# Attention weights all in two halves, the threshold on ScalarE, and a new order of the attention's operations

## The chip, the core and the metric

The kernel runs on one core of a Trainium2 chip. The metric is the device time of one execution in microseconds (us), here the median of several. The core has TensorE (PE; its weight loads are listed apart as PEld), VectorE (DVE), ScalarE (ACT), GpSimd (POOL) and SyncE (SP, which here only issues transfers).

## What is computed

The reference has three stages: attention in which only scores close to the row's largest one count, a mixture of experts that gives each token to one expert, and a feed-forward layer. The change is in the attention.

```python
def _attn_ref(q, k, v, tau) -> np.ndarray:      # (4, 8, 576, 64) each
    scale = 1.0 / np.sqrt(q.shape[-1])
    scores = scale * np.matmul(q, k.transpose(0, 1, 3, 2))
    thresh = np.max(scores, axis=-1, keepdims=True) - tau
    scores = np.where(scores >= thresh, scores, -1000000000.0)
    scores = scores - np.max(scores, axis=-1, keepdims=True)
    attn = np.exp(scores)
    attn = attn / (np.sum(attn, axis=-1, keepdims=True) + 1e-09)
    return np.matmul(attn, v).astype(np.float32)
...
    attn_out = _attn_ref(**attn_kwargs)
    x = np.ascontiguousarray(attn_out.transpose(0, 2, 1, 3)).reshape(B * S, H * D)
    x = _moe_ref(x=x, **moe_kwargs)
    return _moe2_ref(x=x, **moe2_kwargs)
```

## The kernel before

The attention works in 16 pairs: a pair is one head of two of the four batch rows, 2 x 576 = 1152 queries, cut into nine tiles of 128 (tile 4 holds 64 queries of each row and needs twice the products). For each tile `qk` puts the negated, scaled scores s (128 x 576) into one of two score buffers in PSUM; `smin` takes the least of each row on VectorE (column 0 of a small tile mx, whose column 1 holds tau); `sthr` adds tau to it (column 2); `sexp` makes e = exp(least - s) on ScalarE; `smask` on VectorE keeps e where s is at most column 2, writes the weights p and sums each row. The score buffer is free when the mask is done.

TensorE then turns p by 128 x 128 transposes into a PSUM bank t (`ptr`; two banks, for one or two tiles at a time). From there the turned weights go to SBUF (`evac`) and are multiplied with v (`pv`, four products a pair, each 288 queries wide, one bank v). A product in float32r is made exact enough by two halves: hi is the value rounded, lo is what the rounding dropped, and v has its two halves side by side as the stationary operand `hlv`, so that one pass with `pth` (hi) and one with `ptl` (lo) multiply all of it. The keys come in five blocks, four of 128 and one of 64. In the kernel before, `NAT = (1, 1)` says that one 128-key block of each batch row is not split: it stays float32 in the tile `pt` and is multiplied as a whole float32 product with the unsplit `rawv`. The other blocks' halves are made in one of three ways: hi by ScalarE and lo by VectorE from PSUM; a copy to SBUF (tile x) by ScalarE and both halves on GpSimd, for the groups that `VIA` names; or, for the second block, both halves on GpSimd from `pt`. The 64-key block keeps its two halves in `pt4`. `oout` copies a product's result to o, and `fin` folds the two halves of v and adds the experts' logits; `fin_l` and `fin_x` scale them by the row sums.

The order of all this is not the order of the code. `pair` hands every operation to a planner (`Plan`) with its engine, a cost, its dependencies, the buffers that it takes and a rank; the planner lists them by earliest start, and among equals by rank. The numbers of `BIAS` (by kind of operation) and `BIASP` (by kind and pair) are added to the ranks. Each engine then works through its own list in that order. After the last pair the routing follows (`pick`, `count`, `slot`, and `scatter`, which writes the tokens to the experts' rows), and after it the experts and the feed-forward layer, which the change doesn't touch.

Of the kernel before, what the change touches and what calls it, by code (L numbers as in the profile page):

```python
# [16 lines left out]
ALU = mybir.AluOpType  # L17
# [135 lines left out]
def attn_moe_ffn(ctx: ExitStack, tc, q, k, v, tau, emb, mtau, w1, w2, w_in, w_out, alpha, out):  # L153
# [192 lines left out]
    COL = [0, 256, 512, 640, 896]  # L346
    PQ = []

    def load(pr, nm):
# [212 lines left out]
    C0 = min(NAT)  # L562

    def dst(pr, tag):
        st = PQ[pr]
        if tag not in st:
            shp = {"pt": [128, 2, 2 * S], "pt4": [128, 2 * S]}.get(tag, [128, 4 - C0, 2 * S])
            st[tag] = new(tag, shp, F32 if tag == "pt" else F32R)
        return st[tag]

    def evac(pr, g, chunks, what):
# [12 lines left out]
        v = m[:, 0:len(chunks) * n].rearrange("p (c j) -> p c j", c=len(chunks))  # L584
# [1088 lines left out]
```

## Time and profile before

| | us |
|---|---|
| median of three executions | 1065.36 (1065.16 to 1066.11) |
| profiled execution, its own time | 1063.56 |
| span from its first to its last instruction | 1061.4 |
| busy in the span: TensorE | 1008.0 (95%) |
| VectorE | 708.5 (67%) |
| ScalarE | 507.6 (48%) |
| GpSimd | 529.0 (50%) |

The attention takes about the first 375 us of the span, the routing, the experts and the feed-forward layer the rest. Busy time is the time in which an engine has at least one instruction under way; a TensorE that is busy can have instructions that wait for one another. A share of the whole span mixes stages, so the rows further down are cut by stage.

### The profile page before, as it was taken

Reading aid. Unit: us, or ns where it says so; the run is one execution under the profiler, and the core shown is the slowest. Engines: PE = TensorE matmul, PEld = TensorE weight load, DVE = VectorE, ACT = ScalarE, POOL = GpSimd, SP = SyncE. Lnnn points to the kernel's source line nnn. Section 1 sums busy time; section 2 is a strip of 40 time slices with the busy share of each in tenths; the row PEclk is TensorE's granted clock in tenths of the full one; section 3 lists DMA queues with packets and bytes.
Section 4 is the critical chain, followed back from the end, with each engine's and each line's share of the span. In section 5 each row is a group of like instructions: output and inputs, shape, how many; then the busy total and the mean of one; then the engine's idle time right before and its main releaser. Section 6 shows DMA issues by size and latency. Waiting matters only on the chain. (4 is left out here: it accounts for less than half of the span.)

```text
span 1061.4 us, 17732 instructions
## 1 busy us (share of the span) xinstructions
PE 1008.0 (95%) x6224; PEld 908.6 (86%) x6224; DVE 708.5 (67%) x1501; ACT 507.6 (48%) x1074; POOL 529.0 (50%) x610
## 2 busy tenths in 40 slices
PE   7999999999999849999999997999999999999995
PEld 6888888878888738999999996999999999999995
DVE  8988888898889747787868887889642222422321
ACT  5777777788777534555546553232231111311112
POOL 6688786888886432222355223756533222332223
PEclk9999999999999979999999998999999999999998
DMA  4265564433321066686988854222220000000001
GB/s 117 66 186 164 155 170 139 120 116 89 80 67 40 1 200 226 191 266 180 242 204 195 246 166 111 80 63 77 80 90 30 1 1 1 31 30 1 1 1 63
DMA packets 100098, 113.67 MB, mean 107 GB/s; under 512 B 22072, under 2 KB 81464, under 8 KB 100000
## 3 DMA queue, kind: packets, MB, share of 16 engines
q1 hardware_dynamic: 96544, 102.99, 34.5%
q0 software_dynamic: 3456, 9.46, 2.4%
q8 instruction: 51, 0.84, 0.3%
q14 instruction: 47, 0.39, 0.1%
HBM read 75.21 MB, written 28.36 MB: 98 GB/s over the span
## 5 line engine op out<-in xcount | busy, mean ns | idle before, releaser
L1560 POOL TENSOR_TENSOR gl<-t,gh 128x384 fp32r<-128x384 f32 x96 | 102.5, 1068 | 246.5 <-ACT gh L1559 246.5
L1556 DVE TENSOR_SCALAR t<-h,alpha_t 128x384 f32<-128x384 f32 x96 | 59.1, 616 | 206.2 <-PE h L1554 200.7
L1559 ACT CAST gh<-t 128x384 fp32r<-128x384 f32 x96 | 49.3, 513 | 271.3 <-DVE t L1557 162.8
L530 DVE TENSOR_REDUCE mx<-s 128x1 f32<-128x576 f32 x144 | 108.1, 754 | 25.5 <-PE s L523 24.1
L546 DVE SCALAR_TENSOR_TENSOR p<-s,mx,e 128x576 f32<-128x576 f32 x144 | 115.9, 810 | 10.8 <-ACT e L539 7.8
L539 ACT ACTIVATE e<-s,mx 128x576 f32<-128x576 f32 x144 | 107.2, 746 | 14.9 <-DVE mx L530 13.6
L1004 DVE TENSOR_TENSOR w<-stg,w 128x512 fp32r<-128x512 f32 x128 | 107.8, 858 | 9.1 <-ACT w L1003 8.5
L1572 PE MATMUL o<-wo,gl 128*128 128x512 f32 x288 | 113.3, 394 | 0.0
L1571 PE MATMUL o<-wo,gh 128*128 128x512 f32 x288 | 113.1, 393 | 0.0
L1570 PE MATMUL o<-wo,gh 128*128 128x512 f32 x288 | 112.3, 390 | 0.0
L559 PE MATMUL t<-ident,p 128*128 128x128 f32 (+1 forms) x720 | 107.6, 277 | 3.6 <-DVE ptl L377 1.1
L559 PEld LDWEIGHTS t<-ident,p 128*128 128x128 f32 (+1 forms) x720 | 80.9, 137 | 7.5 <-ACT pt L586 3.4
L523 PE MATMUL s<-ks,qs 128*128 128x288 f32 x256 | 80.6, 330 | 6.2 <-DVE p L546 5.3
L1003 ACT CAST w<-stg 128x512 fp32r<-128x512 f32 x128 | 76.7, 619 | 15.8 <-DMA stg<-in_moe_w_dram 15.8
L1097 PE MATMUL y<-h,w 128*128 128x256 f32 (+6 forms) x256 | 80.2, 313 | 2.8 <-DVE h L1065 2.8
L1096 PE MATMUL y<-h,w 128*128 128x256 f32 (+6 forms) x256 | 82.3, 321 | 0.0
L1060 PE MATMUL l<-x,w 128*128 128x256 f32 (+6 forms) x256 | 79.8, 312 | 0.3 <-DVE x L1048 0.2
L1059 PE MATMUL l<-x,w 128*128 128x256 f32 (+6 forms) x256 | 79.9, 312 | 0.0
L1098 PE MATMUL y<-h,w 128*128 128x256 f32 (+6 forms) x256 | 79.6, 311 | 0.0
L1061 PE MATMUL l<-x,w 128*128 128x256 f32 (+6 forms) x256 | 79.5, 310 | 0.0
L523 PE MATMUL s<-kx,qs 128*128 128x288 f32 x256 | 72.9, 299 | 0.2
L1554 PE MATMUL h<-yh,wi_b 128*128 128x384 f32 x216 | 73.0, 338 | 0.0
(233 smaller groups left out, 2756.1 us busy)
## 6 DMA issues: line engine op xcount, KB each, us to landing
stg<-in_moe_w_dram SPq DMA_DIRECT2D x64, 512.0 KB, 5.4
kx<-ks SPq DMA_DIRECT2D x60, 144.0 KB, 2.5
xd<-zt SPq DMA_DIRECT2D x8, 1024.0 KB, 7.5
raw<-in_moe_w_in_dram SPq DMA_DIRECT2D x16, 512.0 KB, 3.7
raw<-in_moe_w_out_dram SPq DMA_DIRECT2D x16, 512.0 KB, 3.5
rawk<-in_k_dram SPq DMA_DIRECT2D x16, 256.0 KB, 2.9
rawq<-in_q_dram SPq DMA_DIRECT2D x16, 256.0 KB, 2.9
yd<-zt SPq DMA_DIRECT2D x4, 1024.0 KB, 6.8
```

What stands on the lines that cost most here:

```text
L523: nc.tensor.matmul(s[:, hf, 0:288], lt, st[nm, a][:, hf * 288:(hf + 1) * 288], start=(j == 0 and x == 0), stop=(j == n - 1 and x == 1))
L530: nc.vector.tensor_reduce(out=mx[:, 0:1], in_=st["s", t][:, :, 0:288], op=ALU.min, axis=AX.XY)
L539: nc.scalar.activation(e, st["s", t][:, :, 0:288], AF.Exp, bias=st["mx", t][:, 0:1], scale=-1.0)
L546: nc.vector.scalar_tensor_tensor(out=p.rearrange("q (a b) -> q a b", a=2), in0=st["s", t][:, :, 0:288], scalar=st["mx", t][:, 2:3], in1=st ...
L559: nc.tensor.transpose(m[0:w, j * n + i * 128:j * n + (i + 1) * 128], st["p", t][:, c * 128:c * 128 + w], ident)
L1004: nc.vector.tensor_tensor(t[:, 1], src, t[:, 0].bitcast(F32), op=ALU.subtract)
L1096: nc.tensor.matmul(m[:, 0:n], w[:, 0, dsl], h[:, 0, 0:n], start=(f == 0), stop=False)
L1097: nc.tensor.matmul(m[:, 0:n], w[:, 0, dsl], h[:, 1, 0:n], start=False, stop=False)
L1560: nc.gpsimd.tensor_tensor(gl, g, gh.bitcast(F32), op=ALU.subtract)
L1570: nc.tensor.matmul(m, gh[:, ts], WO[f][:, 0, :], start=(f == 0), stop=False)
L1571: nc.tensor.matmul(m, gh[:, ts], WO[f][:, 1, :], start=False, stop=False)
L1572: nc.tensor.matmul(m, gl[:, ts], WO[f][:, 0, :], start=False, stop=(f == KF2 - 1))
```

## The change

All four 128-key blocks of a batch row are now split, so `pt` and the product with `rawv` are gone: a product is nine passes of the same kind. Each transposed bank of 128 x 512 is one unit; the nine units of a pair are named A to I, and B, D, E, G and I are copied by ScalarE and split on GpSimd in every pair, while A, C, F and H have hi from ScalarE and lo from VectorE. `sthr` moves from VectorE to ScalarE. There are two x tiles in place of one and one raw v in place of two. The planner's costs and all of its rank numbers are other ones.

```diff
-VIA = ['04', '01234', '023', '0134', '014', '0134', '02', '134', '01234', '34', '014', '01234', '0134', '014', '03', '123']
...
-NAT = (1, 1)
-BIAS = {'min': -79.2, 'load': 3.4, 'evh': -27.7, 'qk': -15.7, 'mask': -161.5, 'evl': -43.0, 'kx': -23.1, 'evn': 11.0, 'exp': -32.2, 'pv': 9.4, 'fin': 3.6, 'thr': -8.5, 'qkt': -13.6, 'ptr': -2.3, 'finx': 5.3, 'evv': 1.3, 'qko': -1.8, 'split': 27.1, 'oout': 3.3, 'evp': -19.6, 'sumsq': 2.9, 'scat': -18.6, 'slot': -10.9, 'pick': -4.3, 'finz': 13.2, 'count': 11.6, 'finl': -6.5}
+VIA = ['BDEGI', 'BDEGI', 'BDEGI', 'BDEGI', 'BDEGI', 'BDEGI', 'BDEGI', 'BDEGI', 'BDEGI', 'BDEGI', 'BDEGI', 'BDEGI', 'BDEGI', 'BDEGI', 'BDEGI', 'BDEGI']
...
+BIAS = {'min': -474.8, 'load': -7.2, 'evh': -28.3, 'qk': -99.2, 'mask': -184.6, 'evl': -166.8, 'kx': -199.8, 'evn': 11.0, 'exp': -34.2, 'pv': 158.5, 'fin': 3.5, 'thr': -36.3, 'qkt': -13.5, 'ptr': 31.1, 'finx': 5.2, 'evv': 9.6, 'qko': 3.7, 'split': 69.3, 'oout': 15.7, 'evp': -94.0, 'sumsq': 238.1, 'scat': 37.7, 'slot': 158.0, 'pick': 116.5, 'finz': 90.8, 'count': -22.6, 'finl': 8.7, 'zero': -375.8}
...
-    slots = dict(rawk=1, rawq=1, rawv=2, hlk=1, hlq=1, hlv=2, ks=3, qs=3, kx=3, qr=2, s=2, t=2, v=1, m=1, e=2, p=5,
-                 mx=4, z=3, rz=2, pt=2, pth=2, ptl=2, pt4=2, x=1, o=1)
+    slots = dict(rawk=1, rawq=1, rawv=1, hlk=1, hlq=1, hlv=2, ks=3, qs=3, kx=3, qr=2, s=2, t=2, v=1, m=1, e=2, p=5,
+                 mx=4, z=3, rz=2, pth=2, ptl=2, pt4=2, x=2, o=1)
...
+    UNITS = [(0, 0), (0, 2), (1, 0), (1, 2), (2, 0), (3, 0), (3, 2), (4, 0), (4, 2)]
...
     def sthr(pr, t):
         mx = PQ[pr]["mx", t]
-        nc.vector.tensor_reduce(out=mx[:, 2:3], in_=mx[:, 0:2], op=ALU.add, axis=AX.X)
+        nc.scalar.activation(mx[:, 2:3], mx[:, 0:1], AF.Identity, bias=mx[:, 1:2])
...
-        if what == "n":
-            nc.scalar.copy(dst(pr, "pt")[:, :, cols], v[:, 0:2])
+        if what == "raw":
+            st["x", g, chunks] = x = new("x", [128, 512])
+            nc.scalar.copy(x, m)
             return
-        if what in ("hi1", "lo1"):
-            hi_lo("POOL", dst(pr, "pth")[:, 0, cols], dst(pr, "ptl")[:, 0, cols], st["pt"][:, 1, cols])[what == "lo1"]()
-            return
...
-        for c in range(NAT[a]):
-            nc.tensor.matmul(acc[0:64, 0:288], raw[:, blk + c, :], st["pt"][:, c, cols], start=False, stop=False)
-        nc.tensor.matmul(acc[:, 0:288], hl[:, 4 - NAT[0] + a].rearrange("p c d -> p (c d)"), st["pt4"][:, cols],
+        hl = st["hlv"]
+        for c in range(4):
+            lt = hl[:, 6 * a + c].rearrange("p c d -> p (c d)")
+            nc.tensor.matmul(acc[:, 0:288], lt, st["pth"][:, c, cols], start=(c == 0), stop=False)
+            nc.tensor.matmul(acc[:, 0:288], lt, st["ptl"][:, c, cols], start=False, stop=False)
+        nc.tensor.matmul(acc[:, 0:288], hl[:, 4 + a].rearrange("p c d -> p (c d)"), st["pt4"][:, cols],
                          start=False, stop=True)
...
-            th = add("DVE", 0.1, at(sthr, t), (mn,), b + 0.55, use=[bx], kind="thr")
-            ex = add("ACT", 0.63, at(sexp, t), (mn,), b + 0.6, take=[be], use=[bs, bx], kind="exp")
-            mk[t] = add("DVE", 0.73, at(smask, t), (ex, th), b + 0.7,
+            th = add("ACT", 0.21, at(sthr, t), (mn,), b + 0.55, use=[bx], kind="thr")
+            ex = add("ACT", 0.67, at(sexp, t), (mn,), b + 0.6, take=[be], use=[bs, bx], kind="exp")
+            mk[t] = add("DVE", 0.83, at(smask, t), (ex, th), b + 0.7,
...
-            pvs.append(add("PE", 1.1 + 0.245 * NAT[j // 2], at(pv, j), need, b, take=[bv],
-                           use=[buf(t) for t in ("pt", "pth", "ptl", "pt4", "rawv", "hlv")], kind="pv"))
+            pvs.append(add("PE", 1.25, at(pv, j), need, b, take=[bv],
+                           use=[buf(t) for t in ("pth", "ptl", "pt4", "hlv")], kind="pv"))
```

Of the planner's numbers the line `BIAS` stands for the rest (`BIASP` now has numbers for all 16 pairs, before for seven). What they do is seen in the engines' lists.

The first place is TensorE's list in the middle of the attention, around one product v of a pair (numbers behind names tell buffers apart; rows between that are alike are left out). Before:

```order
L397 MATMUL m_4407<-identr_71,hlk_4182 128x128 x4
L612 MATMUL v_4414<-pth_4120,hlv_3949 128x288
L613 MATMUL v_4414<-ptl_4121,hlv_3949 128x288
...
L615 MATMUL v_4414<-pt_4115,rawv_3871 64x288
L616 MATMUL v_4414<-pt4_4153,hlv_3949 128x288
L523 MATMUL s_4431<-ks_4039,qr0_209 128x288
```

Now, at the like place:

```order
L556 MATMUL t_4445<-ident_66,p_4355 128x128
L599 MATMUL v_4453<-pth_4092,hlv_3902 128x288
L600 MATMUL v_4453<-ptl_4093,hlv_3902 128x288
...
L601 MATMUL v_4453<-pt4_4127,hlv_3902 128x288
L556 MATMUL t_4469<-ident_66,p_4288 64x128
L520 MATMUL s_4478<-ks_4115,qs_4290 128x288
```

The row with the whole float32 operands pt and rawv is gone; the pair of rows hi and lo stands four times in place of three.

The second place is the work of two score tiles early in the attention, on ScalarE and on VectorE. ScalarE before and now (o, x, pt and pt4 are evacuations, ks and qs those of the next pair's keys and queries):

```order
L539 ACTIVATE e_1620<-s_1577,mx0_213 128x576
L623 COPY o_1633<-v_1604 128x288
L411 ACTIVATE qs_1652<-m_1641,qneg_116 128x512
L586 COPY pt_1405<-t_1646 128x2x256
L539 ACTIVATE e_1674<-s_1627,mx1_214 128x576
L594 COPY x_1690<-t_1654 128x512
```

```order
L531 ACTIVATE mx0_213<-mx0_213 128x1
L536 ACTIVATE e_1472<-s_1429,mx0_213 128x576
L531 ACTIVATE mx1_214<-mx1_214 128x1
L536 ACTIVATE e_1491<-s_1452,mx1_214 128x576
L582 COPY x_1499<-t_1474 128x512
L608 COPY o_1315<-v_1481 128x288
```

VectorE before and now:

```order
L546 SCALAR_TENSOR_TENSOR p_1591,z0_217<-s_1538,mx3_216,e_1574 128x576
L530 TENSOR_REDUCE mx0_213<-s_1577 128x1
L582 TENSOR_TENSOR pt4_1438<-t_1594,pt4_1438 64x256
L534 TENSOR_REDUCE mx0_213<-mx0_213 128x1
L640 TENSOR_REDUCE rz_1624<-z0_217 128x9
L641 RECIPROCAL rz_1624<-rz_1624 128x9
L546 SCALAR_TENSOR_TENSOR p_1639,z1_218<-s_1577,mx0_213,e_1620 128x576
```

```order
L527 TENSOR_REDUCE mx0_213<-s_1429 128x1
L576 TENSOR_TENSOR pt4_1457<-t_1438,pt4_1457 64x256
L527 TENSOR_REDUCE mx1_214<-s_1452 128x1
L376 TENSOR_TENSOR ptl_1403<-t_1441,pth_1402 128x2x256
L543 SCALAR_TENSOR_TENSOR p_1497,z0_217<-s_1429,mx0_213,e_1472 128x576
L543 SCALAR_TENSOR_TENSOR p_1504,z0_217<-s_1452,mx1_214,e_1491 128x576
```

The small row that writes mx from mx has left VectorE (L534) and stands on ScalarE (L531) ahead of the exponential of its tile; on VectorE a lo half (ptl) of 512 columns stands more often between the tiles' rows.

The third place is TensorE's list at the end of the last pair: m is the first part of `fin`, s with oh is the routing's `count`, v the third of the four products. Before:

```order
L632 MATMUL m_5613<-fold_147,o_5587 128x72 x4
L612 MATMUL v_5619<-pth_5397,hlv_5332 128x288
L613 MATMUL v_5619<-ptl_5398,hlv_5332 128x288
...
L616 MATMUL v_5619<-pt4_5433,hlv_5332 128x288
L828 LDWEIGHTS tri_83
L828 MATMUL s_5643<-oh1_121,tri_83 128x40
```

Now:

```order
L617 MATMUL m_5576<-fold_147,o_5545 128x72 x4
L556 MATMUL t_5587<-ident_66,p_5507 64x128
L556 MATMUL t_5587<-ident_66,p_5548 64x128
L809 LDWEIGHTS tri_83
L809 MATMUL s_5603<-oh1_121,tri_83 128x40
...
L599 MATMUL v_5617<-pth_5371,hlv_5164 128x288
```

The third product stood between `fin` and `count`; now it stands behind `count`.

## Rows read from the trace of the kernel before

**Rows 1.** Windows of the span, all engines: busy us, instructions, TensorE clock, transfers.

```profile
core 0: us, PE busy (x) PEld busy (x) DVE busy (x) ACT busy (x) POOL busy (x), PEclk, DMA share, GB/s
75.00:340.00 265.00, 257.92 (x1899) 221.03 (x1899) 229.03 (x597) 207.37 (x453) 211.25 (x281) 1.00 0.42 118
340.00:375.00 35.00, 31.99 (x217) 25.60 (x216) 25.77 (x75) 21.34 (x47) 17.83 (x27) 1.00 0.03 8
400.00:1061.00 661.00, 641.14 (x3615) 597.60 (x3613) 378.64 (x619) 218.74 (x448) 239.91 (x199) 0.99 0.35 102
```

**Rows 2.** Groups by line and shape, 75 to 340 us: count, busy us, mean ns, idle before.

```profile
L539 ACT ACTIVATE e<-s,mx 128x576 f32<-128x576 f32 x108 | 80.5, 747 | 7.5 <-DVE mx L530 6.8
...
L375 POOL TENSOR_TENSOR ptl<-x,pth 128x512 fp32r<-128x512 f32 x37 | 47.5, 1285 | 1.3
...
L375 POOL TENSOR_TENSOR ptl<-pt,pth 128x256 fp32r<-128x256 f32 x48 | 35.3, 736 | 1.5
...
L374 POOL TENSOR_SCALAR pth<-x 128x512 fp32r<-128x512 f32 x37 | 23.0, 622 | 12.5 <-ACT x L594 12.1
...
L374 POOL TENSOR_SCALAR pth<-pt 128x256 fp32r<-128x256 f32 x48 | 19.7, 410 | 20.2 <-ACT pt L586 20.1
...
L534 DVE TENSOR_REDUCE mx<-mx 128x1 f32<-128x2 f32 x108 | 15.9, 152 | 2.0
...
L377 DVE TENSOR_TENSOR ptl<-t,pth 128x512 fp32r<-128x512 f32 x11 | 7.4, 677 | 0.7 <-POOL hlq L374 0.7
...
L407 ACT ACTIVATE qr<-m,qneg 128x64 fp32r<-128x64 f32 x24 | 6.5, 333 | 0.0
...
L404 ACT CAST ks<-m 128x64 fp32r<-128x64 f32 x24 | 3.9, 218 | 1.4 <-PE m L397 1.3
L377 DVE TENSOR_TENSOR ptl<-t,pth 128x256 fp32r<-128x256 f32 x9 | 3.8, 422 | 1.4 <-ACT pt L586 0.9 <-issue 0.4
```

**Rows 3.** Timeline of TensorE around one product: start, length in us, instruction.

```profile
208.93 0.29 PE L612 MATMUL v<-pth,hlv 128*128 128x288 f32 x1
...
209.58 0.29 PE L613 MATMUL v<-ptl,hlv 128*128 128x288 f32 x1
209.80 0.70 PE L615 MATMUL v<-pt,rawv 128*64 128x288 f32 x2
210.43 0.40 PE L616 MATMUL v<-pt,hlv 128*128 128x288 f32 x1
210.66 0.29 PE L523 MATMUL s<-ks,qs 128*128 128x288 f32 x1
```

**Rows 4.** Waits, 75 to 340 us: us in total, times, longest.

```profile
PEld v L616 <- issue: 21.0, 48, 0.4
DVE mx L530 <- PE s L523: 15.5, 30, 2.3
...
PEld v L615 <- issue: 7.7, 47, 0.2
DVE p L546 <- ACT e L539: 7.3, 14, 1.4
```

**Rows 5.** TensorE alone in windows near the start: us, busy us, granted clock.

```profile
22.00:24.00 2.00, 1.08 (x9) 1.00 0.16 35
24.00:26.00 2.00, 0.76 (x10) 1.00 0.98 229
...
28.00:30.00 2.00, 2.00 (x13) 0.50 0.28 82
```

**Rows 6.** Timeline of TensorE at the end of the last pair.

```profile
368.25 1.10 PE L632 MATMUL m<-fold,o 128*128 128x72 f32 x8
369.15 0.38 PE L612 MATMUL v<-pth,hlv 128*128 128x288 f32 x1
...
370.74 0.40 PE L616 MATMUL v<-pt,hlv 128*128 128x288 f32 x1
371.62 0.18 PE L828 MATMUL s<-oh,tri 128*128 128x40 bf16 x1 [0.48 <-DVE oh L821]
```

More of the change, by code (lines that the diff above doesn't have):

```diff
@@ L140, in t_act @@
 def t_act(n):
-    return 0.05 + n / 1200
+    return 0.08 + n / 1090
 def t_dve(n):
-    return 0.07 + n / 960
+    return 0.09 + n / 870
 def t_pool(n, lo):
-    return 0.16 + n / (481 if lo else 1196)
+    return 0.16 + n / (430 if lo else 1100)
 @with_exitstack
@@ L381, in split @@
         raw = st["raw" + nm]
-        if nm == "v":
-            raw = raw[:, NAT[0]:10 - NAT[1]]
         if not half:
@@ L560, in ptr @@
                                     st["p", t][:, c * 128:c * 128 + w], ident)
-    C0 = min(NAT)
     def dst(pr, tag):
@@ L566, in dst @@
         if tag not in st:
-            shp = {"pt": [128, 2, 2 * S], "pt4": [128, 2 * S]}.get(tag, [128, 4 - C0, 2 * S])
-            st[tag] = new(tag, shp, F32 if tag == "pt" else F32R)
+            st[tag] = new(tag, [128, 2 * S] if tag == "pt4" else [128, 4, 2 * S], F32R)
         return st[tag]
@@ L583, in evac @@
             return
-        v = m[:, 0:len(chunks) * n].rearrange("p (c j) -> p c j", c=len(chunks))
-        if what == "n":
-            nc.scalar.copy(dst(pr, "pt")[:, :, cols], v[:, 0:2])
-            return
-        if what in ("hi1", "lo1"):
-            hi_lo("POOL", dst(pr, "pth")[:, 0, cols], dst(pr, "ptl")[:, 0, cols], st["pt"][:, 1, cols])[what == "lo1"]()
-            return
-        v = v[:, len(chunks) - 2:]
-        if what == "raw":
-            st["x", g] = x = new("x", [128, 512])
-            nc.scalar.copy(x[:, 0:2 * n].rearrange("p (c j) -> p c j", c=2), v)
-            return
-        if ("x", g) in st:
-            v = st["x", g][:, 0:2 * n].rearrange("p (c j) -> p c j", c=2)
-        hi, lo = dst(pr, "pth")[:, 2 - C0:, cols], dst(pr, "ptl")[:, 2 - C0:, cols]
-        hi_lo("POOL" if ("x", g) in st else "ACT", hi, lo, v)[what == "lo"]()
+        k = len(chunks)
+        v = m[:, 0:k * n].rearrange("p (c j) -> p c j", c=k)
+        if what == "raw":
+            st["x", g, chunks] = x = new("x", [128, 512])
+            nc.scalar.copy(x, m)
+            return
+        x = st.get(("x", g, chunks))
+        if x is not None:
+            v = x.rearrange("p (c j) -> p c j", c=k)
+        hi, lo = (dst(pr, nm)[:, chunks[0]:chunks[0] + k, cols] for nm in ("pth", "ptl"))
+        hi_lo("ACT" if x is None else "POOL", hi, lo, v)[what == "lo"]()
     def pv(pr, j):
@@ L606, in pv @@
         acc = st["v", j]
-        hl, raw = st["hlv"], st["rawv"]
-        blk = [0, 10 - NAT[1]][a]
-        first = [0, 6 - NAT[0]][a]
-        for i, c in enumerate(range(NAT[a], 4)):
-            lt = hl[:, first + i].rearrange("p c d -> p (c d)")
-            nc.tensor.matmul(acc[:, 0:288], lt, st["pth"][:, c - C0, cols], start=(i == 0), stop=False)
-            nc.tensor.matmul(acc[:, 0:288], lt, st["ptl"][:, c - C0, cols], start=False, stop=False)
-        for c in range(NAT[a]):
-            nc.tensor.matmul(acc[0:64, 0:288], raw[:, blk + c, :], st["pt"][:, c, cols], start=False, stop=False)
-        nc.tensor.matmul(acc[:, 0:288], hl[:, 4 - NAT[0] + a].rearrange("p c d -> p (c d)"), st["pt4"][:, cols],
+        hl = st["hlv"]
[4 more added lines that the diff above has]
+        nc.tensor.matmul(acc[:, 0:288], hl[:, 4 + a].rearrange("p c d -> p (c d)"), st["pt4"][:, cols],
                          start=False, stop=True)
@@ L688, in pair @@
             ld[nm] = add("DMA", 4.6 if nm == "v" else 3.4, at(load, nm), (), base + off, take=[buf("raw" + nm)], kind="load")
-        for nm, off, n in (("k", -14, 576), ("q", -13.5, 576), ("v", -2, D * (10 - sum(NAT)))):
+        for nm, off, n in (("k", -14, 576), ("q", -13.5, 576), ("v", -2, D * 10)):
             if pr == 0 and nm != "v":
@@ L779, in pair @@
             bm = buf("m", ("f", part))
-            f = add("PE", 0.203 * (4 + part), at(fin, part), oo[0:2 + 2 * part] + emb_op, b, take=[bm], use=[buf("o")],
+            f = add("PE", 0.05 + 0.224 * (4 + part), at(fin, part), oo[0:2 + 2 * part] + emb_op, b, take=[bm], use=[buf("o")],
                     kind="fin")
```

34 lines of the change are left out of this document (14 added, 20 removed).

## The prediction

> **What bounds the kernel now.** I first cut the span by stage [rows 1]. Everything that the change touches lies ahead of 375 us; the 661 us behind 400 are to be left as they are. So I read the middle of the attention, 75 to 340 us, where the pairs repeat. The groups by line [rows 2] show 108 exponentials there, nine to a pair: 12 pairs in 265 us, 22.08 us a pair. In the windows [rows 1] TensorE is busy for 257.92 of the 265 us (21.5 a pair, 0.6 idle), VectorE for 229.03 (19.09), GpSimd for 211.25 (17.60), ScalarE for 207.37 (17.28). TensorE bounds this stage, with VectorE close behind. A busy TensorE need not be at work, so I looked at what its instructions wait for [rows 4]: the two longest of its entries are waits for "issue" at lines 616 and 615, 21.0 and 7.7 us. They stand at one place, the whole float32 product and the pass behind it.
>
> **TensorE: the whole product goes.** The timeline of one product [rows 3] gives its price. Six passes of hi and lo start from 208.93 to 209.58, 0.13 us apart. From the last of them to the next group (210.66) are 1.08 us, for that pass, the whole product and the pass at line 616. Two passes at 0.13 leave 0.82 us for the whole product. It holds the waits for issue: 28.7 us over 48 products is 0.60 each [rows 4], so it costs TensorE far more than its columns. In its place come two passes, 0.26 us. The saving is 0.56 us a product, 2.24 a pair, 35.8 us for 64 products. The other bound is nothing, if the waits for issue only cover time that TensorE would wait anyway for another engine; I take the full 0.56 for TensorE's own list, since the next group follows at once [rows 3], and look for what swallows it on the other engines.
>
> The Trainium skill, "FP8 and Floating Point Precision", section "TensorE Precision Notes", says that a true FP32 product takes four passes through the array. By that rule the product would cost 4 x 0.13 = 0.52 us, the saving would be 0.26 and 64 of them 16.6 us, less than half. The trace has 0.82, and I go by the trace.
>
> **VectorE: a small instruction out, large ones in.** Out go nine threshold additions a pair at 0.152 us [rows 2]: 1.37. Lo halves from PSUM cost 0.677 us for 512 columns and 0.422 for 256; in the 12 pairs there are 11 and 9 of them, 0.94 us a pair. Now there are four of 512 in every pair, 2.71. The sum is 19.09 - 1.37 - 0.94 + 2.71 = 19.5 us a pair. If the threshold additions were hidden beside their neighbours and give nothing back, it is 20.9.
>
> **ScalarE: nine thresholds in.** The trace has no ScalarE instruction of one column. The nearest rows [rows 2] are a cast of 64 columns (3.9 us over 24, 0.16 each as it adds to the busy time) and a scaled one of 64 with a per-row operand, which the threshold has too (6.5 over 24, 0.27). Nine of them are 1.5 to 2.4 us a pair; I take 0.27, the row with the operand. That makes 17.28 + 2.4 = 19.7; the copies stay what they are, but for one 512-wide copy in place of two narrow ones.
>
> **GpSimd.** A pair had four hi/lo splits of 256 from pt (0.410 + 0.736) and 37/12 of 512 (0.622 + 1.285): 10.5 us; now five of 512, 9.5 [rows 2]. The split of v grows from 512 to 640 columns, a quarter of 1.9, 0.5. GpSimd stays at about 17 and is no bound.
>
> **SP and the buffers.** The load of v has one issue fewer, and its single raw buffer now waits for GpSimd's split in place of the last product. I cost this at nothing: what hides it is that a pair's v is wanted only once half of its tiles are turned, about half of 22.08 us after its first. If that cover fails, a product waits for a transfer.
>
> **The end.** In the last pair the third product moves behind `count` [rows 6]. It took 1.8 us (369.15 to the row of line 616 at 370.74, plus its 0.23), most of the time in which `count` waited for VectorE's routing; it still had 0.48 us left to wait. Now `count` waits alone and nine passes, 1.2 us, come later. Three earlier or later products are 0.56 shorter, 1.7. The two about cancel: 0, give or take 1.5.
>
> **The sum.** TensorE with its present idle time needs 22.08 - 2.24 = 19.84 us a pair, ScalarE 19.7, VectorE 19.5, GpSimd 17. Three in-order engines that hand each tile to and fro can't all be full, so the saving isn't had whole. VectorE now waits 15.5 us for scores and 7.3 for exponentials in 12 pairs [rows 4], 1.3 and 0.6 a pair. A shorter TensorE list makes scores earlier: I keep the wait for exponentials, since ScalarE gets fuller, and half of that for scores. 19.5 + 0.6 + 0.65 = 20.75 us, 1.33 less than now, and 21.3 for 16 pairs. On the profiled execution's 1063.56 us (2.2 more than its span) that gives 1042.3. It lay 1.8 below the median of the runs, so the median should be **1044 us**; between 1034 and 1057 I call this case right. Chance 0.56.
>
> **Rivals.**
> - *The whole saving arrives.* The new order is planned with costs nearer to the traced ones, and busy times count overlaps: TensorE's 19.84 then stays the bound. For it: TensorE is the fullest engine in every row of the attention [rows 1]. Against: ScalarE and VectorE within 0.4 us. 35.8 us less: 1030. Chance 0.22, and 0.04 more for still less, below 1025, if the order also removes waits.
> - *The threshold's detour (slower).* Before, the addition ran on VectorE while ScalarE took the exponential. Now both stand on ScalarE between a tile's least score and its mask, the threshold ahead, behind whatever copies were listed earlier; behind a mask that waits stand the next tile's minimum, lo halves and `fin_x`, and for the mask's score buffer waits TensorE. If this puts more than 1.33/9 = 0.15 us a tile on VectorE's idle time, nothing is gained. A threshold of 0.27 that isn't hidden for five tiles of six is 0.23 a tile: 20.75 + 2.07 = 22.8, 11.8 us more than now, 1077. For it: masks already wait for exponentials, 14 of 108 [rows 4]. Against: VectorE has other work to do between a minimum and its mask. Chance 0.09.
> - *The clock.* Near the start TensorE was busy for 1.84 of 4 us, and then its granted clock was 0.50 of full speed, the lower of its two levels, 1.2 GHz in place of 2.4 [rows 5]. If an emptier list brings that on in the attention, each 2 us at that clock cost up to 1 us; ten such windows in the attention take 10 us of the gain: 1054. Against: at 32.0 of 35 us busy, late in the attention, the clock was still 1.00 [rows 1], and the forecast leaves TensorE 19.84 - 0.6 of 20.75 us, a like share. Chance 0.05. The Trainium skill, "TensorE: Matmul & The Clock Gate", section "A second HAM failure mode: psum-queue depth-cycling", says that short idle stretches between groups of products can set the clock going up and down; by that rule this rival would be likelier, and the row at 1.00 speaks against it.
> - *No change*, all of the time given up to waits between three full engines: 1063 to 1067. Chance 0.04.
>
> **How the numbers follow.** 0.2%, about 2 us, is what a measurement of this kernel can tell from no change. Faster: 0.56 + 0.22 + 0.04 + 0.05 = 0.87; the same 0.04; slower 0.09. The range for 8 in 10 runs from the first rival's 1030 less 5 for its unknown order, 1025, to the forecast's 1057 and a little beyond, 1060; outside lie the detour, no change, and the case below.
>
> **What would show it.** Some 115 exponentials in 265 us of the attention's middle in place of 108 (265/20.75 x 9). No wait for issue in the products, and 1.2 us from a product's first pass to the next group. VectorE's four lo halves a pair at 0.68 us, and its busy time at 94% of the stage against 86% now. ScalarE's one-column instruction at 0.2 to 0.3 us, and its busy share near 95%. The forecast is wrong if VectorE's wait for exponentials grows beyond the 0.6 us a pair kept here, if TensorE waits for masks or transposed weights instead of for issue, or if the stages behind 400 us move.

## The result, and the profile after

The changed kernel takes 1052.01 us (median of four executions, 1049.34 to 1054.73), beside 1065.55 us for the kernel before: a ratio of 0.9874 [0.9855, 0.9893], 13.5 us less. Its profiled execution took 1054.73 us, the longest of the four, with a span of 1052.9 us.

First the windows by stage, as in [rows 1], with the end of the attention cut finer:

```profile
core 0: us, PE busy (x) PEld busy (x) DVE busy (x) ACT busy (x) POOL busy (x), PEclk, DMA share, GB/s
75.00:340.00 265.00, 251.31 (x2008) 236.67 (x2008) 245.38 (x545) 229.15 (x572) 200.08 (x205) 1.00 0.41 117
340.00:350.00 10.00, 7.68 (x47) 6.99 (x46) 7.53 (x21) 5.73 (x14) 5.29 (x6) 0.83 0.00 0
350.00:375.00 25.00, 9.21 (x54) 8.35 (x51) 10.32 (x44) 8.07 (x24) 10.74 (x11) 0.57 0.33 116
400.00:1052.00 652.00, 629.87 (x3553) 587.14 (x3553) 369.23 (x605) 212.38 (x436) 235.24 (x197) 0.99 0.35 99
```

The groups by line and shape of the same 265 us, which answer to [rows 2] (count, busy us, mean ns, idle before):

```profile
L543 DVE SCALAR_TENSOR_TENSOR p<-s,mx,e 128x576 f32<-128x576 f32 x114 | 91.5, 809 | 7.2 <-ACT e L536 4.8 <-ACT mx L531 1.5
...
L536 ACT ACTIVATE e<-s,mx 128x576 f32<-128x576 f32 x114 | 83.8, 735 | 2.9 <-DVE mx L527 2.8
...
L376 DVE TENSOR_TENSOR ptl<-t,pth 128x512 fp32r<-128x512 f32 x52 | 35.6, 685 | 1.3 <-ACT pth L375 0.7
L531 ACT ACTIVATE mx<-mx 128x1 f32<-128x1 f32 x114 | 34.0, 298 | 3.2 <-DVE mx L527 2.6
```

There are 114 exponentials where 108 stood: 12.67 pairs in 265 us, 20.92 us a pair. Busy per pair that is TensorE 19.84, VectorE 19.37, ScalarE 18.09, GpSimd 15.8. The granted clock of this stretch is 1.00; from 340 to 350 us, still ahead of the last mask, it is 0.83. The timeline of one product, as in [rows 3]:

```profile
204.00 0.38 PE L599 MATMUL v<-pth,hlv 128*128 128x288 f32 x1
204.22 0.29 PE L600 MATMUL v<-ptl,hlv 128*128 128x288 f32 x1
...
205.15 0.29 PE L601 MATMUL v<-pt,hlv 128*128 128x288 f32 x1
205.28 0.29 PE L520 MATMUL s<-ks,qr 128*128 128x288 f32 x1
```

From its first pass to the next group are 1.28 us; in [rows 3] it was 1.73 (208.93 to 210.66). That product was one of the shorter ones: over all products that start between 75 and 340 us the median was 1.83 us before and is 1.27 now, 0.56 less. The waits of the same stretch, as in [rows 4]:

```profile
POOL pth L373 <- ACT x L582: 43.0, 23, 4.3
...
PEld s L520 <- DVE p L543: 8.8, 24, 0.8
...
DVE p L543 <- ACT e L536: 4.8, 15, 0.8
PE s L520 <- DVE p L543: 4.3, 14, 0.8
PEld t L556 <- ACT x L582: 4.2, 9, 1.1
DVE mx L527 <- PE s L520: 3.8, 11, 0.7
```

The kernel before had these waits at the same place:

```profile
PEld s L523 <- DVE p L546: 6.0, 12, 0.9
...
PE s L523 <- DVE p L546: 3.6, 9, 0.8
```

The waits for issue at the product are gone. TensorE waits a little longer for masks, which free a score buffer: 4.3 us in its own list in place of 3.6, and 8.8 us in the list of weight loads in place of 6.0. (The two lists show the same waits in large part and can't be added.) It also waits for ScalarE's copies x. VectorE's two waits of [rows 4], 15.5 and 7.3 us, have shrunk to 3.8 and 4.8. GpSimd's 43 us of waiting belong to an engine that has work for 15.8 of 20.92 us.

Two moments tell where the time came from and where a part of it went: the end of the last mask of pair 15 (VectorE) and the last scatter (GpSimd). The timeline of the kernel before:

```profile
364.12 0.08 DVE L546 DVE_READ_ACCUMULATOR p<-s,mx,e 128x1 f32 x1
...
384.23 0.98 POOL L847 DMA_INDIRECT xd<-x_sb,slot_i  x1 [0.30 <-issue]
```

and of the changed kernel, with VectorE's long wait between them:

```profile
348.48 0.08 DVE L543 DVE_READ_ACCUMULATOR p<-s,mx,e 128x1 f32 x1
...
361.71 0.20 DVE L635 TENSOR_TENSOR Lp<-m,rz 128x40 f32<-128x40 f32 x1 [6.42 <-PE m L617]
...
370.87 0.98 POOL L828 DMA_INDIRECT xd<-x_sb,slot_i  x1 [0.30 <-issue]
```

The last mask ends at 348.56 us in place of 364.20, 15.6 earlier; the last scatter at 371.85 in place of 385.21, 13.4 earlier. What lies between them grew from 21.0 to 23.3 us. Behind the last scatter this execution takes 681.0 us, before it was 676.2; what these 4.8 us are worth the sections on the experiments and on the hardware say. The timeline of TensorE at the end of the last pair, as in [rows 6], shows what grew:

```profile
350.28 1.01 PE L617 MATMUL m<-fold,o 128*128 128x72 f32 x8
...
353.95 0.19 PE L809 MATMUL s<-oh,tri 128*128 128x40 bf16 x1 [2.37 <-DVE oh L802]
...
354.10 0.59 PE L599 MATMUL v<-pth,hlv 128*128 128x288 f32 x1
354.49 0.44 PE L600 MATMUL v<-ptl,hlv 128*128 128x288 f32 x1
354.73 0.44 PE L599 MATMUL v<-pth,hlv 128*128 128x288 f32 x1
...
357.10 0.61 PE L599 MATMUL v<-pth,hlv 128*128 128x288 f32 x1 [0.49 <-ACT o L608]
...
359.43 2.24 PE L617 MATMUL m<-fold,o 128*128 128x72 f32 x10
```

TensorE waits 2.37 us for the routing ahead of `count`, as the changed order has it, and both products behind it run at the clock's lower level: 0.24 us from pass to pass in place of 0.13 (the granted clock of 355 to 360 us is 0.50).

### The profile page after: what moved, and what is told of

The parts are those of the page before. It is cut to its first block, busy times and chain, and to the rows that moved or that the text cites. A ratio compares the mean times of both kernels' runs of the same rounds, so it can differ in the third digit from the quotient of the medians.

```text
span 1052.9 us, 17564 instructions
## 1 busy us (share of the span) xinstructions
PE 984.8 (94%) x6224; PEld 916.6 (87%) x6224; DVE 713.1 (68%) x1394; ACT 524.1 (50%) x1202; POOL 508.8 (48%) x504
## 5 line engine op out<-in xcount | busy, mean ns | idle before, releaser
L374 POOL TENSOR_TENSOR ptl<-x,pth 128x512 fp32r<-128x512 f32 x80 | 103.0, 1288 | 3.5
L373 POOL TENSOR_SCALAR pth<-x 128x512 fp32r<-128x512 f32 x80 | 50.0, 626 | 59.0 <-ACT x L582 58.9
```

The source lines that it names most:

```text
L374: lambda: nc.gpsimd.tensor_tensor(lo, raw, hi.bitcast(F32), op=ALU.subtract))
```

## The experiments

In the table, "a pair" is the time from the end of pair 0's last mask to that of pair 15's, over 15, and "the end" the time from the last mask to the end of the last scatter, both in the profiled execution. The runs stand in three groups, e1 to e4, e5 to e8 and e9 to e11, each beside the kernel before on the same chip (1068.62, 1066.82 and 1066.02 us); e12 has one execution, beside one of 1069.25 us.

| run | median us (executions) | ratio to before | a pair, us | the end, us |
|---|---|---|---|---|
| before | | | 22.03 | 21.0 |
| after | 1052.01 (4) | 0.9874 [0.9855, 0.9893] | 20.92 | 23.3 |
| e1 | 1051.08 (5) | 0.9821 [0.9806, 0.9837] | 20.86 | 21.6 |
| e2 | 1048.17 (5) | 0.9806 [0.9789, 0.9822] | 20.90 | 19.4 |
| e3 | 1080.27 (6) | 1.0096 [1.0078, 1.0113] | 22.58 | 27.4 |
| e4 | 1050.83 (5) | 0.9837 [0.9818, 0.9857] | 20.91 | 19.9 |
| e5 | 1110.24 (5) | 1.0405 [1.0387, 1.0423] | 20.74 | |
| e6 | 1055.54 (6) | 0.9894 [0.9876, 0.9912] | 21.00 | 22.7 |
| e7 | 1048.67 (5) | 0.9844 [0.9823, 0.9865] | 20.53 | |
| e8 | 1089.51 (5) | 1.0220 [1.0200, 1.0241] | 22.79 | 25.1 |
| e9 | 1050.42 (4) | 0.9862 [0.9841, 0.9883] | 20.89 | 20.9 |
| e10 | 1051.50 (4) | 0.9867 [0.9847, 0.9888] | 20.96 | 20.3 |
| e11 | 1051.98 (5) | 0.9871 [0.9847, 0.9895] | 20.91 | 23.3 |
| e12 | 1035.63 (1) | | 20.23 | |

The rows after, e1 and e11 are one kernel, and e1's interval of the ratio doesn't overlap the first one's: between groups, half a per cent of the ratio tells nothing. So the edits are judged by the two columns on the right. The attention of e2, e5, e7 and e12 gives another result, and so another routing: their ends are left out, or, for e2, not used.

The theory: the removal of the whole float32 product from TensorE's list is the gain; less than its 2.24 us a pair arrives because other waits take over. Rivals: the new order makes the gain; the move of the threshold makes or costs it; VectorE, now with larger lo halves, is the new bound.

**e1, the changed kernel once more**, with no edit.

> The changed kernel once more, unaltered, as the mark for the others and to see how far its times scatter. Both theories: 1049 to 1055 us, ratio to before 0.985 to 0.990. If the scatter comes from TensorE's clock at the end of the attention, a faster execution shows fewer microseconds at the lower level there.

1051.08 us (1048.31 to 1051.49), ratio 0.9821, 17.5 us less than before on this chip. The time is inside what was expected; the ratio lies below the 0.985 to 0.990 expected, since the kernel before took longer in this group. The pairs take 20.86 us, 0.06 less than in the first profile; here the granted clock is 1.00 from 340 to 350 us. The end is 1.7 us shorter.

**e2, the product alone.** The kernel before, in its own order, with the whole product replaced by two passes:

```diff
-            nc.tensor.matmul(acc[0:64, 0:288], raw[:, blk + c, :], st["pt"][:, c, cols], start=False, stop=False)
+            lt = hl[:, first].rearrange("p c d -> p (c d)")
+            nc.tensor.matmul(acc[:, 0:288], lt, st["pth"][:, 0, cols], start=False, stop=False)
+            nc.tensor.matmul(acc[:, 0:288], lt, st["ptl"][:, 0, cols], start=False, stop=False)
```

> The kernel before with its own order, in which the whole float32 product is replaced by two passes of the same kind as the others (on the first block's halves, so that block counts twice and the unsplit one not at all). Everything else is as before. Theory 1 (the whole product holds TensorE for 0.82 us and TensorE bounds the attention): TensorE's list is 0.56 us shorter 64 times, 35.8 us; VectorE needs no more than before, so at least half of it arrives: 1030 to 1048 us. Theory 2 (the waits for issue cover time in which TensorE would wait for others anyway; the new order brought the gain): less than 8 us, 1057 or more.

It takes 1048.17 us, a little less than the changed kernel on the same chip and just above the first theory's 1048. One block counts twice, so the result and the routing are other ones, and the attention is what can be compared. Its windows row:

```profile
75.00:340.00 265.00, 250.91 (x1986) 237.25 (x1985) 239.03 (x629) 212.58 (x467) 217.59 (x289) 0.99 0.41 117
```

A pair takes 20.90 us, as in the changed kernel, with ScalarE and GpSimd loaded quite otherwise (212.58 and 217.59 of 265 us against 229.15 and 200.08). So the product's removal alone gives the whole gain of 1.1 us a pair. The run leaves the first block unsplit, so it doesn't pay for that block's halves, which the changed kernel does make; what new order and new units give is at most room for that work.

**e3, the product alone, the other way.** The changed kernel, in its own order, with the fourth block of each product as one whole float32 product:

```diff
+            if c == 3:
+                nc.tensor.matmul(acc[0:64, 0:288], hl[:, 6 * a + c, 0, :].bitcast(F32),
+                                 st["pth"][:, c, cols].bitcast(F32), start=False, stop=False)
+                continue
             nc.tensor.matmul(acc[:, 0:288], lt, st["pth"][:, c, cols], start=(c == 0), stop=False)
```

> The changed kernel with its own order, in which the fourth block of every product is one whole float32 product of its hi half with v's hi half, in place of two passes (both lo halves of that block are left out). Theory 1: TensorE needs 0.56 us more 64 times; it has about 1.1 us of idle time a pair, so 18 to 34 us longer than the changed kernel, 1069 to 1086 us. Theory 2: within 8 us of the changed kernel.

1080.27 us, 29.2 more than e1 on the same chip, and 22.58 us a pair, 1.73 more. One product and its waits:

```profile
215.70 0.29 PE L604 MATMUL v<-ptl,hlv 128*128 128x288 f32 x1
215.92 0.70 PE L600 MATMUL v<-pth,hlv 128*64 128x288 f32 x2
216.55 0.40 PE L605 MATMUL v<-pt,hlv 128*128 128x288 f32 x1
216.79 0.29 PE L520 MATMUL s<-ks,qs 128*128 128x288 f32 x1
```

```profile
PEld v L605 <- issue: 20.6, 47, 0.4
...
PEld v L600 <- issue: 7.6, 47, 0.2
```

From the last lo pass to the next group are 1.09 us, 0.83 without the two passes of 0.13: the price of [rows 3] again, and with it the waits for issue, 28.2 us over 47 products. (The block's lo halves are still made, but not multiplied.) Of the 2.24 us a pair that this puts on TensorE, 1.73 come out as time.

**e4, the third product of the last pair** ahead of `count`, where it stood before:

```diff
-        last_pv[:] = pvs[3:]
+        last_pv[:] = pvs[2:]
...
-                last_pv[0].deps.append(c)
+                last_pv[1].deps.append(c)
+                c.deps.append(last_pv[0])
```

> The changed kernel with the last pair's third product ahead of the routing's count on TensorE. Theory 1 (the end gave back some 2 us because the product waits behind count and then runs at the lower clock): the last scatter ends 1 to 3 us earlier against the last mask, 1048 to 1051 us. Rival (the routing's chain on VectorE sets the end, wherever the product stands): within 1 us of the changed kernel.

The median (1050.83, 1045.38 to 1054.73) can't be told from e1's. The end is 19.9 us in its profile, 1.7 shorter than in e1's and 3.4 shorter than in the first one's, about as the first theory had it. I took this up again in e9.

**e5, less work for VectorE.** The four large lo halves of a pair write 64 of 512 columns, and the products take the first two blocks' hi twice:

```diff
+        if x is None and what == "lo":
+            hi, lo, v = hi[:, :, 0:32], lo[:, :, 0:32], v[:, :, 0:32]
...
-            nc.tensor.matmul(acc[:, 0:288], lt, st["ptl"][:, c, cols], start=False, stop=False)
+            nc.tensor.matmul(acc[:, 0:288], lt, st["ptl" if c > 1 else "pth"][:, c, cols], start=False, stop=False)
```

> The changed kernel with its own order, in which VectorE's four large lo halves of a pair are made for 32 of 256 (64 of 512) columns only; the products read the hi half a second time in their place, so TensorE's and ScalarE's lists are the same, and the two lo blocks are left out of the result. VectorE has some 1.9 us a pair less to do (19.4 to 17.5). Theory 1 (VectorE is now as near its limit as TensorE): 0.5 to 1.0 us a pair shorter, 1035 to 1043 us. Rival (TensorE alone still bounds): within 4 us of the changed kernel, 1047 or more.

The attention's result and the routing are other ones, and what follows takes longer (the feed-forward layer's first product starts at 679.9 us, in the changed kernel at 629.8), for a cause that no run took apart: only the attention is compared.

```profile
75.00:340.00 265.00, 250.78 (x2005) 237.80 (x2003) 226.90 (x546) 229.73 (x575) 201.26 (x206) 0.99 0.41 116
```

A lo half now takes 220 ns in place of 685, 1.9 us a pair; a pair is 0.17 us shorter, in place of the first theory's 0.5 to 1.0. VectorE is not the bound by itself.

**e6, the threshold back on VectorE**, at the same place in the order:

```diff
-        nc.scalar.activation(mx[:, 2:3], mx[:, 0:1], AF.Identity, bias=mx[:, 1:2])
+        nc.vector.tensor_reduce(out=mx[:, 2:3], in_=mx[:, 0:2], op=ALU.add, axis=AX.X)
```

> The changed kernel with its own order, with the threshold's addition back on VectorE, at the same places of the program. VectorE gets 1.4 us a pair more, ScalarE 2.7 us less (its one-column instruction took 0.298). Theory 1 (VectorE near its limit, the detour over ScalarE hidden): 0.5 to 1.4 us a pair longer, 1059 to 1073 us. Rival (the detour holds the masks up): shorter than the changed kernel by 3 us or more.

```profile
75.00:340.00 265.00, 250.19 (x1985) 234.09 (x1985) 249.94 (x653) 210.83 (x455) 201.04 (x205) 1.00 0.41 118
```

A pair takes 21.00 us, 0.08 to 0.14 more than with the threshold on ScalarE, and the ranges of the executions (1051.38 to 1057.32; 1048.31 to 1054.73) overlap. Neither expectation came true: the loss is smaller than the 0.5 us expected at least, and the pair is no shorter. Nine additions raise VectorE's busy time by 0.44 us a pair (249.94 x 21.00 / 265 = 19.81, against 19.37) and take 1.38 from ScalarE's (16.71 against 18.09).

**e7, less work for TensorE.** The products leave out the third and the fourth block:

```diff
-        for c in range(4):
+        for c in range(2):
             lt = hl[:, 6 * a + c].rearrange("p c d -> p (c d)")
```

> The changed kernel with its own order, in which the products leave out the third and fourth 128-key blocks: four passes of 0.13 us less a product, 2.1 us a pair, all on TensorE; the splits are still made. Theory 1 (VectorE as near its limit as TensorE): TensorE's saving arrives for less than half, 0.3 to 0.9 us a pair, 1036 to 1046 us. Rival (TensorE alone bounds): three quarters or more, 1.6 us a pair, below 1027 us.

```profile
75.00:340.00 265.00, 237.85 (x1815) 213.72 (x1814) 248.07 (x553) 229.98 (x578) 202.91 (x208) 0.99 0.41 117
```

```profile
PEld s L520 <- DVE p L543: 21.3, 45, 1.9
PE s L520 <- DVE p L543: 12.2, 26, 1.7
```

16 passes fewer, 2.1 us a pair of TensorE, shorten a pair by 0.39 us, inside the first theory's 0.3 to 0.9. (Two blocks are left out of the result, so the routing is another one and the median says less.) The waits for a score buffer, that is for masks, grow to 12.2 us in TensorE's own list in place of 4.3, and to 21.3 in place of 8.8 in that of the weight loads. So from e3's list to the changed kernel's 2.24 us less on TensorE give 1.7, and the next 2.1 give 0.39.

**e8, the order's numbers.** The changed kernel with the rank numbers `BIAS` and `BIASP` of before; the operations and the planner's costs stay new.

> The changed kernel with the rank numbers of the kernel before (both tables), its new costs kept. Theory 1 (most of the gain is the whole product's removal): within 6 us of the changed kernel, on the longer side, 1050 to 1058 us. Rival (the ranks are what makes room for the fuller VectorE): 8 us or more longer, 1060 or more.

1089.51 us, some 38 more than the changed kernel in the other groups, 22.79 us a pair. The granted clock from 75 to 340 us is 0.97 here, which can be a small part of it. Its waits:

```profile
POOL pth L373 <- ACT x L582: 57.8, 26, 3.8
PEld s L520 <- DVE p L543: 20.9, 33, 2.3
ACT pth L375 <- PE t L556: 17.3, 15, 3.2
...
DVE mx L527 <- PE s L520: 12.1, 25, 1.1
```

The rival's expectation came true: the same instructions in an unfit order lose more than the product's removal gives. Every engine waits, TensorE for masks, VectorE for scores, ScalarE for transposes.

**e9 to e11, the end of the attention.** e9 is the kernel of e4 again, e11 the changed kernel, both in five rounds on one chip; e10 is e9 with eight products that nobody reads ahead of the second part of `count`:

```diff
+            if i == 1:
+                w = hold_s[0]
+                for _ in range(KEEP):
+                    nc.tensor.matmul(w[:, 1, 0:128], ident, ident, start=True, stop=True)
```

> The changed kernel, with the third product of the last pair ahead of count again, as it stood before; timed a second time in five rounds, since its first median could not be told from the changed kernel's. If the clock at the end of the attention is what gave 2 us back (the changed kernel's third and fourth product ran at 0.24 us a pass in place of 0.13 behind a wait of 2.37 us), the fourth product runs at 0.13 us a pass, the last scatter ends about 20 us after the last mask, and the median is 1.5 to 3 us below that of the unchanged kernel on this chip. If the order of the third product doesn't matter, the two medians agree within 1 us.

> As the run before it, with eight extra float32 products of 128 columns, whose result nobody reads, ahead of the second part of count; they fill TensorE's wait for the routing. If a fall of the clock in this wait is what makes the last part of the attention longer, the granted clock stays higher behind them and the last scatter ends up to 1 us earlier than without them. If the wait for the routing sets the end, they change nothing (within 0.5 us of the last mask to the last scatter), or cost up to 1 us where count is ready before they are done.

> The changed kernel unchanged, in five rounds on the same chip, as the measure for the two runs ahead of it: 1051 us by both theories (the two groups of executions so far have medians of 1052.0 and 1051.1), and a clock at the lower level at the end of the attention that begins in one execution or another at a place of its own.

The timeline of TensorE in e9:

```profile
350.16 0.38 PE L599 MATMUL v<-pth,hlv 128*128 128x288 f32 x1
...
352.79 0.18 PE L809 MATMUL s<-oh,tri 128*128 128x40 bf16 x1 [1.21 <-DVE oh L802]
...
354.33 0.41 PE L599 MATMUL v<-pth,hlv 128*128 128x288 f32 x1 [1.26 <-ACT o L608]
354.57 0.30 PE L600 MATMUL v<-ptl,hlv 128*128 128x288 f32 x1
354.70 0.30 PE L599 MATMUL v<-pth,hlv 128*128 128x288 f32 x1
...
355.87 2.24 PE L617 MATMUL m<-fold,o 128*128 128x72 f32 x10
```

and the last row in e4, which is the same kernel:

```profile
356.83 1.54 PE L617 MATMUL m<-fold,o 128*128 128x72 f32 x10
```

In e11 both products run at 0.24 us a pass, as in the changed kernel's first profile, and the end takes 23.3 us. In e9 the third product is done in 1.3 us while `count` waits, the fourth starts at 0.13 us a pass, the clock falls in its last passes, and the end takes 20.9. In e10 the clock stays up through the fourth product and the last `fin` (1.54 us in place of 2.24), and the end takes 20.3. So 2.4 us come from the product's place together with the clock. That e10's extra products kept the clock up is not shown: e4, without them, has the last `fin` at 1.54 us too, and an end of 19.9. What e4, e9 and e10 (19.9 to 20.9) do show, beside the changed order's profiles (23.3, 21.6 and 23.3), is that the end is shorter with the third product ahead of `count`. In the medians little is left of it: 1050.42 (1049.28 to 1051.44) against 1051.98 (1049.38 to 1054.53), with ratios whose intervals overlap. What lies behind the last scatter varies more than that: 675.0 us in e4's profile, 679.1 in e9's, 684.0 in e10's, for the same lists of work. e9 is the best full version here by its median, but not by more than its measurement is uncertain.

**e12, less for both.** e5's and e7's edits in one, with hi alone in the blocks that stay.

> The changed kernel with the two reductions of e5 and e7 in one: VectorE's four large lo halves write 64 of 512 columns, and the products leave out the blocks 3 and 4; the blocks that stay are multiplied with hi alone, so no product waits for a lo half. Results and routing are other ones; compare the attention. A pair then has 1.9 us less of VectorE and 2.1 us less of TensorE than 20.9 us. If those two engines share the bound, so that either alone holds the time up, it falls to 19 us a pair or less. If what is left is the waits from engine to engine in a fixed order (or ScalarE and GpSimd, which keep 18 and 16 us a pair of work), it falls by little more than the sum of the two runs alone, 0.15 and 0.36: 20.3 to 20.5 us a pair.

```profile
75.00:340.00 265.00, 239.73 (x1838) 216.67 (x1837) 230.85 (x562) 232.25 (x585) 204.45 (x211) 0.99 0.41 117
```

The result and the routing are other ones again. A pair takes 20.23 us, 0.69 less than in the changed kernel, with VectorE and TensorE at 17.6 and 18.3 us of busy time a pair. That is just below the 20.3 to 20.5 expected of waits from engine to engine and far from the 19 of a bound that these two share.

## Why the prediction held, and by how much it missed

The forecast was 1044 us, 21.3 less than before; the gain is 13.5, inside the likeliest case's own range of 1034 to 1057 us.

**TensorE's term was right for the product.** 0.56 us a product was forecast, and the median from a product's first pass to the next group fell by 0.56 (1.83 to 1.27; 1.2 forecast); the waits for issue went with it. e2 and e3 show that this removal is the gain. That 19.84 us stands both in the forecast and among the busy times is chance: the forecast's 19.84 held 0.6 us of idle time, so it had 19.24 of work, and the busy time fell from 21.49 to 19.84 only, 1.65 us and not 2.24. Where the other 0.6 us went no run took apart. By the Trainium skill's rule ("FP8 and Floating Point Precision", section "TensorE Precision Notes": four passes for a true FP32 product) e3 would cost 0.26 us a product, at most 1.04 a pair, an estimate with 0.13 us a pass. It cost 1.73, so the trace's 0.82 was the better price.

**The step "the saving isn't had whole" was right; that the sum came so near was partly luck.** The sum was 20.75 us a pair, measured were 20.92, with 114 exponentials for the expected 115. Over 15 pairs that is 1.11 us a pair in place of 1.33, 3.3 us less of a gain. The forecast also counted a 16th pair (1.33 us), while the first pair ended 1.1 us later in this execution. That makes the 15.6 us at the last mask out of 21.3. The luck lies in how the sum was made. It was VectorE's list and two of its waits, 0.6 and 0.65 us. Those two are now 0.38 and 0.30 us a pair (4.8 and 3.8 us over 12.67 pairs), but VectorE stands idle for 20.92 - 19.37 = 1.55 us: its other waits, 0.87 us, the sum put at nothing, though before they were 22.08 - 19.09 - 1.9 = 1.1. And by e5 VectorE's list doesn't hold the pair: 1.9 us less of it gave 0.17.

**Single terms were off and cancelled.** VectorE's sum was 19.5, measured 19.37; but by e6 the nine additions were worth 0.44 us a pair, not 1.37, so the other terms together came out smaller than forecast by as much; which of them, no run took apart. ScalarE's sum was 19.7, measured 18.09: by e6 the nine thresholds cost 1.38, 0.15 each and not the 0.27 taken (its lower bound was 0.16), and the rest of its work fell by 0.6. Accordingly ScalarE is busy for 86% and not 95% of the stage. GpSimd, forecast at about 17 us, has 15.8: the sum left out the narrower splits of before, 14.4 us over 12 pairs, which cost nothing, as GpSimd was no bound.

**The sign of a wrong forecast that did appear.** TensorE waits for masks, as the prediction's last part named, 4.3 us of 265 in its own list; but it did so before, for 3.6. e7 shows more: with shorter products TensorE waits 12.2 us for masks, nearly half of its 27.1 us of idle time, and a pair still takes 20.53 us. VectorE's wait for exponentials did not grow, it fell from 0.6 to 0.4 us a pair. The third sign, that the stages behind 400 us move, came in this execution (4.8 us), but the same lists take 675.0 us behind the last scatter in e4's, less than before's 676.2.

**The term of the end was mis-sized.** It was costed at 0, give or take 1.5: three products shorter against one product later. Measured were 2.3 us more (21.0 to 23.3), outside those bounds. The step left out that TensorE, waiting alone for the routing, could come out of it at the lower clock. In this execution two products of nine passes ran at 0.24 us in place of 0.13, 2.0 us, and the last `fin` took 2.24 in place of 1.54: 2.7 us in all, an estimate from these rows, and enough for the whole miss. In e1 the clock came back in the fourth product, and the end was 21.6; with the third product ahead of `count` it was 19.9, 20.9 and 20.3 (e4, e9, e10). This and the 5.7 us missing at the last mask make up the 8 us between 1044 and 1052.

**The rivals.** The whole saving (1030) is refuted by e7: even with TensorE's list shorter still, a pair stays above 20.5. The threshold's detour (1077) is refuted by e6: away with it, the pair gets no shorter. The clock as a rival inside the attention (1054) gives the right total for the wrong place: from 75 to 340 us the changed kernel's granted clock was 1.00; it fell in the last pair (0.83 from 340 to 350 us) and behind it. In e4 and e9, whose lists are the same up to there, it was 0.99 from 75 to 340 us. All this cost little: e1, at 1.00 up to 350 us, has 20.86 us a pair beside 20.92, 20.91 and 20.89, at most 0.9 us over 15 pairs. Not forecast was e8: that the fit of the order to the operations is worth as much as 1.9 us a pair. The new order does not add to the gain of e2, but the new operations need it.

**Open.** What bounds a pair at 20 to 21 us is known by exclusion. VectorE (e5), TensorE (e7) and both (e12) move it little; ScalarE is 1.4 us a pair emptier in e6 (with VectorE 0.44 fuller) without a gain, and GpSimd 1.4 fuller in e2 (217.59 x 20.90 / 265 = 17.2 against 15.8) without a loss. No run emptied all four engines at once. What is left, argued and not shown, are the waits from one engine's fixed list to the next. No order better than the changed kernel's for its operations was tried, nor a third score buffer.

## What to carry to other kernels

When the fullest engine of a tuned pipeline loses work, don't count the gain down to its own shorter list: here half of 2.24 us a pair arrived, and of a second 2.1 us a fifth. The next engine's list plus its present waits gave a near forecast, but a list that bounds a sum need not bound the kernel: cut it by itself (e5) before you believe it. A saving found by changing one instruction kind may be had without the rest of the change, so build that edit alone (e2) and take it back alone (e3); and when the set of operations changes, an order fitted to the old set must be fitted again, or it costs more than the operations save (e8). Look at what stands behind a wait on TensorE: work moved from ahead of it to behind it can run there at half the clock.

## What the runs showed of the hardware

A short instruction costs an engine less than its length in the trace. ScalarE's threshold is 298 ns long, but the next one starts 0.18 us behind it, here in the changed kernel's timeline:

```profile
121.49 0.28 ACT L531 ACTIVATE mx<-mx 128x1 f32<-128x1 f32 x1
121.67 0.73 ACT L536 ACTIVATE e<-s,mx 128x576 f32<-128x576 f32 x1
```

In busy time it came to 0.15 us (e6), and VectorE's addition of 152 ns to 0.05. The Trainium skill, "ScalarE: Activation LUTs", section "What ACT_TABLE_LOAD costs", gives such an instruction with a per-row bias 280 ns and says that neighbours overlap by some 93 ns. The trace agrees with both: 298 ns, and 0.28 us of which 0.18 pass until the next one starts.

TensorE's clock at the end of the attention differed with what stood ahead. After 2.37 us of waiting for the routing the passes of the third product came 0.24 us apart (granted clock 0.50 from 355 to 360 us; in e1 from the second pass on); after a wait of 1.21 us and one of 1.26 us (e4, e9) they came 0.13 apart, in e4 to the end and in e9 for the first six passes. The length of the wait doesn't settle it alone: in the kernel before, `count`'s second part came at 377.60 us after 2.48 us of waiting, and the granted clock was still 1.00 there. And the time behind the last scatter differed by up to 9 us (675.0 to 684.0) between executions of the same lists, more than several of the edits were worth, for a cause that no run took apart; for changes to the attention, its own rows decided more than the medians.
